# Shared homes for keys, values and folded sums, and 1280 instead of 768 columns of one output unit kept in SBUF

## Chip, cores and metric

One core of a Trainium2 chip. The metric is the device time of one launch in microseconds, the median of several runs. The core's engines are TensorE (PE, with its weight loads shown as PEld), VectorE (DVE), ScalarE (ACT), GpSimd (POOL) and SyncE (SP), and 16 DMA engines move data between HBM and SBUF. [...]

## What is computed

A layernormed input of 2048 rows goes through two branches, whose results are added to the input: a dense network with GELU, and an attention with a recurrent memory. The second is what this text is about: 64 segments of 32 rows, and eight memory rows that each segment takes from the output of the one before it.

```python
for s in range(n_seg):                       # 64, one after the other
    h = concatenate([mem, xs])               # 8 + 32 rows of 1024
    q, k, v = h @ Wq, h @ Wk, h @ Wv         # each 1024 x (32 heads x 128)
    p = softmax(mask(q @ k.T * scale))
    o = (p @ v) @ Wo                         # 4096 x 1024
    mem = o[:8]
    outs.append(o[8:])
return x + concatenate(outs) + dense(xn)
```

In bfloat16 the four weights hold 32 MB. They are read again in each segment, and not all of them fit in SBUF beside the rest.

## The kernel before

**Stages.** Until about 427 us the layernorm and the dense network run. They leave, for each segment, its turned rows and its residual in HBM. Then comes the recurrence, one segment after the other.

**Units.** The four weights are cut into 64 units of 128 x 2048 (512 KB): for each of K, Q and V eight slices of the model dimension in two halves u of 16 heads, and 16 units of Wo, two heads of the 32 each. `ORDER` is the order of use: K half 0, Q half 0, K half 1, Q half 1, V half 0, V half 1, output. 46 units stay in SBUF. 18 are marked S in `PLACED`. Two of these (`KEPT`) lie in four PSUM banks, from which VectorE copies them into a slot (L246). The other 16 are streamed from HBM in every segment by SP, through six slots: `unit_done` (L699) gives a slot back when the unit's matmuls are issued, and `start_stream` (L248) starts the next transfer into it. That transfer waits until TensorE has read the slot. One streamed output unit, `PART`, is partly resident: its first `PART_COLS` columns lie in `half_home`, only the rest is streamed (L257) into the right-hand part of the slot. `PART` is output unit 13 of 16.

**Left rows.** A segment's turned input has 32 columns: 24 of its rows (NX) and the eight memory rows. The last eight rows of each segment ("left" rows) are gathered over four segments (GRP) into a group of 32 and multiplied apart, each product in another segment of the group. With i4 = s mod 4: left K half 0 in i4 = 3 and half 1 in i4 = 0, left Q halves in 1 and 2, left V halves in 0 and 3, left outputs in 1. Where a pass has a left product, each unit is used twice, so its time doubles.

**A half pass** (`half_pass`, L757) goes through the eight units of a half. For each, `product` (L733) issues four matmuls of 128 x 512 with 32 columns of weights, in four column tiles of TensorE (L739). After a unit it may call functions that are listed for that step in `at`: so small work is put between the units by hand. The accumulators are three PSUM banks, `acc`; `mixed` is one more bank for scores, sums, masks and the memory.

**From pass to values.** A K or Q half is copied out of PSUM by ScalarE (`rows_out`, L790) and turned by VectorE (L804, L1007). `scores(u)` (L840) multiplies keys by queries into `mixed` (L848 for the segment, L854 for the left rows), takes Exp on ScalarE into `pr_all` (L860) and masks on VectorE (L867). `sums(u)` (L870) sums over the keys with small matmuls (L875, L881), takes Ln and two Exp on ScalarE (L886, L889) and multiplies on VectorE into `pd_main` (L896) and `pd_left` (L900). A V half is copied out of PSUM by ScalarE (`values_out`, L794). `values(u, rs)` (L907) multiplies it by `pd` (L915, L921) and copies the result out, r = 0 on ScalarE and r = 1 on VectorE (L929), into `outs[u]`. Output units 0 to 7 read the outputs of u = 0, units 8 to 15 those of u = 1 (`o_product`, L944, matmuls L962). In segments without left outputs, units 0 to 8 sum up in column-tile pairs, which `fold` (L971) adds between units 8 and 9 into `folded`. At the end `o_sb` is made (L1081 or L1084), `put_mem` (L284) writes the memory rows into the next segment's input, and the residual is added (L1104).

**Homes.** `d_oL` and `b_oL` (1024 columns each) are the outputs of u = 0 and u = 1: 64 columns for each of 16 heads, of which 32 are for left rows and the rest for the segment's. While they are not yet outputs, parts of them serve as `nat_home` (columns 32 to 63 of each head in `d_oL`: keys of half 1, and `o_sb`) and `q_home` (columns 24 to 63 in `b_oL`: queries). One more tile of 512 columns, tag "a", holds in turn the keys of half 0, the values of half 0, the values of half 1, and the folded sums. `hr_home` holds the turned rows and the residual of a segment.

**Order around the change.** In a segment: K0, Q0, K1, then the Q1 pass with scores(0) after its step 0 and sums(0) after step 6; V0, whose copy follows at once; the V1 pass with scores(1) after step 0, values(0) after step 1 and sums(1) after step 4 (in i4 = 3, where the pass is double: values(0) in two parts after 1 and 3); the output units with values(1) after unit 5 (in two parts after 4 and 6 where V1 has left products).

Of the kernel before, what the change touches and what calls it, by code (L numbers as in the profile page):

```python
# [57 lines left out]
PART_COLS = 768  # L58
# [31 lines left out]
def kernel(  # L90
# [49 lines left out]
    half_home = nc.alloc_sbuf_tensor_at("half_home", [P, DM], BF16, offset=SCRATCH)  # L140
    hr_home = nc.alloc_sbuf_tensor_at("hr_home", [P, 512], BF16, offset=SCRATCH + 2048)
    pd_main = nc.alloc_sbuf_tensor_at("pd_main", [P, 320], BF16, offset=SCRATCH + 3072)

    part_home, pr_all, res_home = half_home[:, 0:PART_COLS], half_home[:, PART_COLS:DM], hr_home[:, 256:512]
# [5 lines left out]
    pd_left = consts.tile([P, 128], BF16, name="pd_left")  # L150
# [66 lines left out]
    def fetch(t, unit):  # L217
        w, i, u = unit
        if unit == PART:
            h = 4 * i + 2 * u  # L220
            nc.sync.dma_start(out=t[:, 0:DM - PART_COLS], in_=Wo_v[:, h, PART_COLS:])
            nc.sync.dma_start(out=t[:, DM - PART_COLS:], in_=Wo_v[:, h + 1, :])
# [57 lines left out]
    b_oL = sp.tile([P, 1024], BF16, name="b_oL")  # L280
    outs = [t.rearrange("p (h t) -> p h t", h=16) for t in (d_oL, b_oL)]
    nat_home, q_home = outs[0][:, :, 32:64], outs[1][:, :, 24:64]
# [19 lines left out]
    with tc.tile_pool(name="ma", bufs=2) as ma, tc.tile_pool(name="mps", bufs=6, space=PSUM) as mps:  # L302
# [95 lines left out]
        def keep_xT(tg, xnT):  # L398
            xl = [sp.tile([P, 2, KT, GRP, NL], BF16, name="xl", tag=("a", "kL0")[k]) for k in range(2)]
# [28 lines left out]
        def turn_R(ttg, eng, small=None):  # L428
# [3 lines left out]
            for i in range(4):  # L432
# [8 lines left out]
                if with_left(seg):  # L441
                    m0 = main_row(slot)
# [4 lines left out]
                if seg < 2:  # L447
                    rows_at.append(NL * (slot ^ 2))
                elif seg >= NSEG - 2:
                    rows_at.append(main_row(1) + SEG + NL * slot)  # L450
# [64 lines left out]
        for tg in range(4):  # L515
            last = tg == 3
            if last:
# [4 lines left out]
                nc.sync.dma_start(out=half_home[:, :], in_=Wo_v[:, h, :])  # L522
# [122 lines left out]
    with tc.tile_pool(name="late", bufs=1) as late, \  # L645
# [69 lines left out]
        for s in range(NSEG):  # L715
# [14 lines left out]
            m0 = main_row(slot)  # L730
# [75 lines left out]
            def turn_k(ps, u):  # L806
                st["kT", u] = sp.tile([P, 16, 32], BF16, name="kT", tag="a")[:, :, :]
                turn(ps, st["kT", u], nc.scalar.copy)
# [31 lines left out]
            def scores(u, meanwhile=None):  # L840
# [4 lines left out]
                for c in range(4):  # L845
# [6 lines left out]
                    for j in range(4):  # L852
# [5 lines left out]
                        )  # L858
                pr = pr_all[:, 0:224]
# [10 lines left out]
            def sums(u):  # L870
# [17 lines left out]
                for b in (1, 0):  # L888
# [5 lines left out]
                pdB = pd_left.rearrange("p (c b a q) -> p c b a q", c=4, b=2, q=NL)  # L894
# [5 lines left out]
                nc.vector.tensor_tensor(  # L900
                    out=pdB.rearrange("p c b a q -> p b c a q"),
                    in0=prB.rearrange("p c (a q) -> p c a q", q=NL)[:, None, :, :, :].to_broadcast([P, 2, 4, 2, NL]),
# [106 lines left out]
            if not first:  # L1009
                at[6] = [lambda: sums(0)]  # L1010
# [164 lines left out]
```

## Time and profile before

| what | value |
|---|---|
| median of 3 runs | 1844.56 us (1840.67 to 1846.51) |
| the profiled execution | 1839.26 us, its span 1837.5 us |
| TensorE clock granted, mean | 0.996 |
| PE busy | 1717.9 us, 93% |
| PEld / DVE / ACT / POOL busy | 49% / 52% / 36% / 15% |
| until the recurrence, 0 to 427 us | DMA share 0.50, 157 GB/s |
| recurrence, 427 to 1837.5 us | DMA share 1.00, 387 GB/s |
| DMA queue of SP | 588.05 MB of 612.94 MB |

The share of a busy engine is an average. For the recurrence it has to be read from its own stretch, by segment or by group of four segments, since the four segments of a group do different amounts of left work. Matmuls overlap in the records. A DMA share over 1 means that packets overlap a little at their ends. In a list of waits a row gives engine, line and tile, what it waited for, the sum in us, how often, and the longest.

### The profile page before, as it was taken

The page shows a single profiled execution, that of the slowest core. Times are in us where ns is not written, and L with a number is a line of the kernel's source. Part 1 is how long each engine was busy: PE and PEld are TensorE (multiplying, and loading weights), DVE is VectorE, ACT ScalarE, POOL GpSimd, SP SyncE. Part 2 cuts the span into 40 slices and gives each one's busy share as a digit, 9 for nine tenths or more (in the row PEclk, how much of TensorE's full clock was granted, in tenths as well). Part 3 has the DMA queues.
Part 4 walks back from the last instruction along what each step waited for, and adds up shares of the span by engine and source line. Part 5 has one row for each costly group of instructions (what it writes and reads, how often), then busy time and mean ns, then how long its engine had stood idle before and what let it go on. Part 6 is the DMA issues. An engine that isn't in the chain of part 4 may idle for free.

```text
span 1837.5 us, 69927 instructions
## 1 busy us (share of the span) xinstructions
PE 1717.9 (93%) x30556; PEld 893.2 (49%) x30576; DVE 955.3 (52%) x2330; ACT 663.8 (36%) x1429; POOL 284.4 (15%) x559
## 2 busy tenths in 40 slices
PE   8999999998999999999999999999999999999997
PEld 4444444444454445454545545454545454545444
DVE  7657483805454545555454555455545454545543
ACT  6334251602333333333333333333333333333333
POOL 0000001501342111111111111112111111111111
PEclk9999999999999999999999999999999999999999
DMA  9931212769999999999999999999999999999998
GB/s 286 313 98 46 55 44 57 260 209 371 397 404 389 391 384 389 381 394 388 373 397 386 400 385 394 374 390 401 389 384 390 383 398 391 397 376 384 389 393 313
DMA packets 229278, 612.94 MB, mean 334 GB/s; under 512 B 46795, under 2 KB 76027, under 8 KB 228972
## 3 DMA queue, kind: packets, MB, share of 16 engines
q1 hardware_dynamic: 207252, 588.05, 84.3%
q0 software_dynamic: 17408, 17.69, 3.0%
q8 instruction: 239, 3.92, 0.8%
q10 hardware_dynamic: 4312, 2.73, 0.5%
q14 instruction: 67, 0.55, 0.1%
HBM read 594.40 MB, written 29.23 MB: 339 GB/s over the span
## 4 chain that ended last, share of the span: by engine, by line
PE 32%; DMA 18%; DVE 4%; ACT 2%; issue 1%; POOL 0%; DVEq 0%; ACTq 0%; SPq 0%
PE acc L739 22%; DMA u<-Wc_K 10%; PE acc L962 6%; DMA outL_d<-half_home 3%; DMA u<-Wc_O 3%; ACT mixed L889 1%; DVE b_oL L804 1%; PE acc L915 1%; DMA hr_home<-hr_d 1%; DVE pd_main L896 1%; PE mixed L848 1%; DMA u<-Wc_V 1%; ACT mixed L886 1%; DMA u<-Wc_Q 0%; PE mixed L854 0%
## 5 line engine op out<-in xcount | busy, mean ns | idle before, releaser
L739 PE MATMUL acc<-u,hr_home 128*32 128x512 bf16 x11520 | 770.8, 380 | 34.0 <-DMA u<-Wc_K 18.2
L739 PEld LDWEIGHTS <-hr_home 128*32 128x32 bf16 x12288 | 342.1, 96 | 317.3 <-issue 57.3
L739 PE MATMUL acc<-u,hrL 128*32 128x512 bf16 x2880 | 248.8, 379 | 3.0 <-DVE folded L978 3.0
L468 PE MATMUL ps<-u 128*128 128x512 bf16 (+1 forms) x920 | 195.7, 375 | 2.0 <-ACT u L388 2.0
L246 DVE TENSOR_SCALAR u<-kept 128x512 uint32<-128x512 uint32 x254 | 163.5, 685 | 35.4 <-PE acc L962 12.3
L962 PE MATMUL acc<-u,d_oL 128*32 128x512 bf16 (+1 forms) x1792 | 153.3, 381 | 11.7 <-DMA u<-Wc_O 9.4
L790 ACT CAST kT<-acc 128x512 bf16<-128x512 f32 x64 | 37.4, 585 | 307.6 <-PE acc L739 307.5
L589 PE MATMUL ps<-u 128*128 128x512 bf16 x657 | 146.2, 379 | 0.8
L962 PEld LDWEIGHTS <-b_oL 128*32 128x32 bf16 (+1 forms) x3381 | 108.4, 98 | 74.5 <-issue 35.9
L896 DVE TENSOR_TENSOR pd_main<-half_home,mixed 128x320 bf16<-128x320 bf16 x128 | 62.4, 487 | 153.2 <-ACT mixed L889 153.2
L468 PEld LDWEIGHTS <-u 128*128 128x128 bf16 x920 | 90.5, 99 | 105.5 <-issue 2.4
L1137 POOL DMA_DIRECT2D out_dram<-hr_home x188 | 96.3, 512 | 294.1 <-DVE hr_home L1104 280.5
L962 PE MATMUL acc<-u,b_oL 128*32 128x256 bf16 (+2 forms) x2062 | 117.1, 289 | 20.2 <-DMA u<-Wc_O 19.5
L804 DVE STREAM_TRANSPOSE b_oL<-b_oL 128x512 bf16<-128x512 bf16 x128 | 90.6, 708 | 64.8 <-ACT b_oL L790 64.8
L268 POOL DMA_DIRECT2D hr_home<-hr_d x58 | 32.8, 565 | 581.3 <-PE acc L739 576.1
L962 PEld LDWEIGHTS <-d_oL 128*32 128x32 bf16 (+1 forms) x2048 | 70.3, 99 | 84.7 <-issue 28.0
L739 PEld LDWEIGHTS <-hrL 128*32 128x32 bf16 x3072 | 82.9, 96 | 51.2 <-issue 7.7
L790 ACT CAST b_oL<-acc 128x512 bf16<-128x512 f32 x128 | 75.1, 587 | 86.1 <-PE acc L739 86.1
L589 PEld LDWEIGHTS <-u 128*128 128x128 bf16 x672 | 65.3, 98 | 77.3 <-DVE g_u L550 0.4
L889 ACT ACTIVATE mixed<-mixed,small_consts 128x160 f32<-128x160 f32 x256 | 94.2, 368 | 8.4
L542 ACT ACTIVATE g_xb<-ps,b1col 128x512 bf16<-128x512 f32 x112 | 76.8, 686 | 55.5 <-PE ps L468 54.7
L794 ACT CAST v<-acc 128x512 bf16<-128x512 f32 x128 | 75.1, 587 | 48.9 <-PE acc L739 48.6
(129 smaller groups left out, 2011.6 us busy)
## 6 DMA issues: line engine op xcount, KB each, us to landing
u<-Wc_K SPq DMA_DIRECT2D x320, 512.0 KB
u<-Wc_V SPq DMA_DIRECT2D x256, 512.0 KB
u<-Wc_O SPq DMA_DIRECT2D x256, 512.0 KB
u<-Wc_Q SPq DMA_DIRECT2D x128, 512.0 KB
u<-Wc_O SPq DMA_DIRECT2D x64, 320.0 KB
u<-in_B_w_dram SPq DMA_DIRECT2D x28, 512.0 KB
hr_home<-hr_d POOLq DMA_DIRECT2D x58, 128.0 KB, 5.5
u<-in_A_Wq_dram SPq DMA_DIRECT2D x14, 512.0 KB
```

The costliest lines, as they stand in the source:

```text
L246: nc.vector.tensor_single_scalar(out=out, in_=in_, scalar=0, op=ALU.bitwise_or)
L468: nc.tensor.matmul(ps[:, SEG * s0:SEG * s1].rearrange("p (s t) -> p s t", t=SEG), lhsT=w1_sb[fb // 2][:, kt, (fb % 2) * P:(fb % 2 + 1) * P ...
L542: nc.scalar.activation(out=xb[:, :], in_=ps[:, :], func=ACT.Identity, bias=b1col[:, fb:fb + 1], scale=1.0)
L589: nc.tensor.matmul(ps[:, :], lhsT=gts[fc // 4][:, fc % 4, t * P:(t + 1) * P], rhs=w2_sb[fc // 2][:, fc % 2, cs], start=(fc == 0), stop=(fc ...
L739: nc.tensor.matmul(o, lhsT=lhs[:, i, :], rhs=m, start=(i == seq[0]), stop=(i == seq[-1]), tile_position=(0, 32 * j),)
L790: cp(out=out, in_=ps.rearrange("p (h e) -> p h e", e=32))
L794: cp(out=t[:, :], in_=ps[:, :])
L804: nc.vector.transpose(out=home, in_=home)
L889: nc.scalar.activation(out=mixed[:, 160 * b:160 * b + 160], in_=mixed[:, 0:160], func=ACT.Exp, scale=-1.0, bias=off[:, b:b + 1],)
L896: nc.vector.tensor_tensor(out=pdA.rearrange("p c b q -> p b c q"), in0=prA[:, None, :, :].to_broadcast([P, 2, 4, 40]), in1=dd, op=ALU.mult,)
L962: nc.tensor.matmul(acc[r0:r0 + rows, c:c + wide], lhsT=lhs[:, 4 * (i % 4) + 2 * u + k, :], rhs=cols, start=start, stop=stop, tile_position ...
L1137: nc.gpsimd.dma_start(out=out_flat[rows, 256 * j:256 * j + 256], in_=res[32 * j:32 * j + NX, :])
```

## The change

It moves the homes and some steps, and lets more columns of `PART` stay.

- `PART_COLS` is 1280 instead of 768. `half_home` has 1536 columns (1280 for the unit, 256 for `pr_all`); `hr_home` moves to another pool. The streamed rest of `PART` is 768 columns.
- The tag "a" is gone. Keys of half 0 and the folded sums go to `nat_home`. `b_oL` is replaced by `q_all` (640 columns) and `left_outs` (512, left outputs of u = 1). Values of both halves, the segment's outputs of u = 1 (`outM`) and `o_sb` share columns 0 to 511 of `q_all` with the queries, one after the other; in i4 = 3 the values of half 1 lie in `kL[1]`.
- `pd_left` is gone: for u = 1 it is in columns 512 to 639 of `q_all`, for u = 0 in a part of `left_outs`, written by two products instead of one.
- scores(0) is issued after the last unit of K1 instead of after step 0 of Q1; its Exp and masks, now `exps`, come before K1's copy. sums(0) comes after step 4 instead of 6, but for i4 = 2.
- V0's copy is issued after the matmuls of scores(1) and before its Exp (`attend`). values(0) comes after step 4, sums(1) after step 6; in i4 = 3 values(0) after 3 and 5, sums(1) after 5, values(1) after units 5 and 7.
- For u = 1 the copy out of `values` has two parts, left rows and segment rows. In segments with left outputs the later eight output units use 32 columns of weights from each of two tiles instead of 64 from one.

```diff
-PART_COLS = 768
+PART_COLS = 1280
...
-    half_home = nc.alloc_sbuf_tensor_at("half_home", [P, DM], BF16, offset=SCRATCH)
-    hr_home = nc.alloc_sbuf_tensor_at("hr_home", [P, 512], BF16, offset=SCRATCH + 2048)
+    half_home = nc.alloc_sbuf_tensor_at("half_home", [P, PART_COLS + 256], BF16, offset=SCRATCH)
...
-            nc.sync.dma_start(out=t[:, 0:DM - PART_COLS], in_=Wo_v[:, h, PART_COLS:])
-            nc.sync.dma_start(out=t[:, DM - PART_COLS:], in_=Wo_v[:, h + 1, :])
+            nc.sync.dma_start(out=t, in_=Wo_v[:, h + 1, PART_COLS - DM:])
...
-    b_oL = sp.tile([P, 1024], BF16, name="b_oL")
-    outs = [t.rearrange("p (h t) -> p h t", h=16) for t in (d_oL, b_oL)]
-    nat_home, q_home = outs[0][:, :, 32:64], outs[1][:, :, 24:64]
+    left_outs = sp.tile([P, 512], BF16, name="left_outs")
+    q_all = sp.tile([P, 640], BF16, name="q_all")
+    outs0, outL = d_oL.rearrange("p (h t) -> p h t", h=16), left_outs.rearrange("p (h t) -> p h t", h=16)
+    v_home = q_all[:, 0:512]
+    outM = v_home.rearrange("p (h t) -> p h t", h=16)
+    nat_home, q_home = outs0[:, :, 32:64], q_all.rearrange("p (h t) -> p h t", h=16)
...
             def turn_k(ps, u):
-                st["kT", u] = sp.tile([P, 16, 32], BF16, name="kT", tag="a")[:, :, :]
-                turn(ps, st["kT", u], nc.scalar.copy)
+                st["kT", u] = nat_home
+                turn(ps, nat_home, nc.scalar.copy)
...
+                if u:
+                    pdB = q_all[:, 512:640].rearrange("p (c b a q) -> p c b a q", c=4, b=2, q=NL)
+                else:
+                    pdB = outL[:, :, 24:32].rearrange("p (c b a) q -> p c b a q", c=4, b=2)
...
-                    out = outs[u][:, 8 * r:8 * r + 8, NL * slot:NL * slot + 40]
-                    cp(out=out.rearrange("p (b c) q -> p c b q", b=2), in_=oV[r])
+                    h = slice(8 * r, 8 * r + 8)
+                    if u == 0 and m0 == NL * slot + NL:
+                        parts = [(outs0[:, h, NL * slot:NL * slot + 40], 0, 40)]
+                    else:
+                        parts = [
+                            ((outL if u else outs0)[:, h, NL * slot:NL * slot + NL], 0, NL),
+                            (outM[:, h, :] if u else outs0[:, h, m0:m0 + SEG], NL, 40),
+                        ]
+                    for out, q0, q1 in parts:
+                        cp(out=out.rearrange("p (b c) q -> p c b q", b=2), in_=oV[r][:, :, :, q0:q1])
...
                     if left_o:
-                        tiles = [(64 * r, 64, (2 * r, 2 * r + 1)) for r in range(2)]
+                        lhs = [(0, 32, outL[:, h, :]), (32, 32, main)] if i >= 4 else [(0, 64, outs0[:, h, :])]
+                        tiles = [(64 * r + r0, w, (2 * r, 2 * r + 1), lhsT) for r0, w, lhsT in lhs for r in range(2)]
...
-                t = sp.tile([P, 256], F32, name="folded", tag="a")
+                t = nat_home.bitcast(F32)
...
-            psK1, psK1L = half_pass("K", 1, left_k[1], {})
+            psK1, psK1L = half_pass("K", 1, left_k[1], {7: [lambda: scores(0)]})
+            exps(0, None if first else lambda: q_left(1))
             st["kT", 1] = nat_home
             rows_out(psK1, nat_home, nc.scalar.copy)
             at = {
-                0: [lambda: scores(0, None if first else lambda: q_left(1)), lambda: nc.vector.transpose(out=nat_home, in_=nat_home)],
+                0: [lambda: nc.vector.transpose(out=nat_home, in_=nat_home)],
             }
             if not first:
-                at[6] = [lambda: sums(0)]
+                at[6 if i4 == 2 else 4] = [lambda: sums(0)]
...
-            st["V", 0] = values_out(psV, sp.tile([P, 512], BF16, name="v", tag="a"), nc.scalar.copy)
...
-            at = {0: [lambda: scores(1)], 4: [lambda: sums(1)]}
+
+            def attend():
+
+                scores(1)
+                st["V", 0] = values_out(psV, v_home, nc.scalar.copy)
+                exps(1)
+
+            at = {0: [attend]}
             if left_v[1]:
-                at.update({1: [lambda: values(0, (0,))], 3: [lambda: values(0, (1,))]})
+                at.update({3: [lambda: values(0, (0,))], 5: [lambda: values(0, (1,)), lambda: sums(1)]})
             else:
-                at[1] = [lambda: values(0, (0, 1))]
+                at.update({4: [lambda: values(0, (0, 1))], 6: [lambda: sums(1)]})
...
-            st["V", 1] = values_out(psV1, sp.tile([P, 512], BF16, name="v", tag="a"), nc.scalar.copy)
+            apart = left_v[1] and not first
+            v1 = kL[1].rearrange("p h t -> p (h t)") if apart else v_home
+            st["V", 1] = values_out(psV1, v1, nc.scalar.copy)
...
-                o_sb = nat_home
+                o_sb = outM
```

## The prediction

> **What bounds the kernel now.** I read the slices first, then the busy row of a long stretch of the recurrence, then who waits for whom, then the timeline of one segment.
>
> ```profile
> PE   8999999998999999999999999999999999999997
> ...
> PEclk9999999999999999999999999999999999999999
> DMA  9931212769999999999999999999999999999998
> ```
>
> From about slice 10 on the 64 segments run, with TensorE and the 16 DMA engines both at nine tenths. The first 427 us are layernorm and the dense network, which the change hardly enters. To part the two, the row for 506 to 1735 us (56 segments, 14 groups of four):
>
> ```profile
> core 0: us, PE busy (x) PEld busy (x) DVE busy (x) ACT busy (x) POOL busy (x), PEclk, DMA share, GB/s
> ...
> 506.20:1735.00 1228.80, 1141.80 (x25054) 613.65 (x25046) 626.40 (x1512) 439.65 (x1023) 206.96 (x395) 1.00 1.01 389
> ```
>
> A group takes 1228.8/14 = 87.8 us. TensorE is busy for 81.6 of it and idle for 6.2. The DMA share is 1.01; cut into slices of 1 us, the packet records give 1.027 on three slices of four, so 1.027 is "full" and the engines miss only 1.6 us a group. DMA work alone is 86.2 us a group. What TensorE waits for (600 to 1800 us):
>
> ```profile
> PE acc L962 <- DMA u<-Wc_O: 24.8, 51, 1.3
> PE acc L739 <- DMA u<-Wc_K: 17.1, 30, 1.9
> PE mixed L848 <- DVE b_oL L804: 10.1, 37, 0.4
> ```
>
> The first two are 41.9 us in 1200, or 3.1 us a group. So TensorE with its own waits needs 87.8 - 3.1 = 84.7 us a group, DMA 86.2, and the group takes 87.8: **the weight stream binds, with TensorE 1.5 us a group behind it.** By segment (i4 = s mod 4): nearly all DMA waits come late in i4 = 0 (its last products and the next segment's first keys) and late in i4 = 2; i4 = 1 and 3, which do more left products, have next to none.
>
> Here the Trainium skill (Perfetto Trace Analysis, Identifying the Most-Contended Engine) speaks for a choice: matmul busy time is no measure of headroom, because matmuls are pipelined. By the busy row (93%) TensorE would be the bound and the removed bytes worth nothing; by the rule that row proves nothing, and the PEld row (50%) leaves room. By the row the sum below would be +14 us (the new TensorE waits alone), by the rule -11. The DMA share and the waits side with the rule.
>
> **Removed bytes.**
>
> ```profile
> u<-Wc_O SPq DMA_DIRECT2D x64, 320.0 KB
> ```
>
> This transfer becomes 192 KB, the other 15 per segment (512 KB) stay. Its 128 packets shrink from 2560 to 1536 bytes. The trace's packet records give 105 ns (mean) for the first size and 65 ns for the second (it occurs in the load phase). Eight packets per engine: 8 x 40 = 0.32 us a segment, x64 = **20.6 us**, or 1.3 us a group; 128 KB at 389 GB/s would be 0.34. Once, in segment 0, 128 KB more are loaded (+0.3 us); in the load phase 128 KB less are copied, beside TensorE work.
>
> **Moved keys.** scores(0) now stands one unit (four matmuls, 0.217 us) earlier. It had 0.32 to 0.76 us between the end of the query transpose and its start, needs 0.05: free. Exp now precedes the copy of K1; that copy feeds only scores(1), some 4 us later. In i4 = 2 Exp waits for a left-output DMA as before, and K1's copy and the transpose wait behind it; the next taker of that PSUM bank is V0, a double pass (3.5 us) later: free. sums(0) is two units earlier in i4 = 0, 1, 3, so net one unit nearer to scores(0): 1.32 us instead of 1.54, with the mask ready 1.20 us after scores(0) starts (1.33 in i4 = 3): at most 0.06 us of wait, in i4 = 3. The gain: Ln, two Exp and then Q1's copy on ScalarE run earlier, and scores(1), which waits for that query transpose (the L804 row above), gets it some 0.23 us sooner in i4 = 1. In i4 = 0 and 3 a left-key copy (0.59) stands before Ln, and the split `pd` product costs VectorE two of about 0.18 (96- and 64-element L867: 198 and 180 ns) instead of one of 0.28, so nothing is gained: +0.1 in i4 = 3. Folded sums in `nat_home` and outputs in `v_home` keep engine and size: nothing.
>
> **Values, where waits are added.** ScalarE in V1/O of an i4 = 0 segment:
>
> ```profile
> 1058.20 0.29 ACT L886 ACTIVATE mixed<-mixed 128x160 f32<-128x160 f32 x1 [0.51 <-PE mixed L881]
> 1058.52 0.77 ACT L889 ACTIVATE mixed<-mixed,small_consts 128x160 f32<-128x160 f32 x2
> 1059.21 0.59 ACT L794 CAST v<-acc 128x512 bf16<-128x512 f32 x1
> 1060.46 0.42 ACT L929 CAST b_oL<-acc 128x320 bf16<-128x320 f32 x1 [0.66 <-PE acc L921]
> ```
>
> and TensorE at the same place:
>
> ```profile
> 1057.82 0.24 PE L875 MATMUL mixed<-half_home,small_consts 128*32 128x160 bf16 x4
> ...
> 1059.97 0.21 PE L915 MATMUL acc<-pd_main,v 64*128 64x80 bf16 x2
> ...
> 1061.03 0.62 PE L962 MATMUL acc<-W_O,b_oL 128*32 128x512 bf16 x12
> ```
>
> V0's copy must now wait until scores(1) has read the queries, and it stands ahead of Exp on ScalarE. Exp(1), its masks and sums(1) queue behind it: Exp moves by about 0.55 us. sums(1) stands two units later (0.43) and had 0.33 to 0.5 us of slack, so it just fits; values(0), at step 4, meets the copy within 0.05 us. Then the chain: sums(1) at 1057.82 to values(1) at 1059.97 is 2.15 us, set by ScalarE (Ln, two Exp, V1's copy, ending at 1059.80). Before, nine units and the sums (2.05 us) lay beside it; now seven (1.62). **TensorE waits 0.43 us more** in i4 = 0. In i4 = 2 as much, where DMA waits of about 0.7 us already lie in that stretch. In i4 = 1 the doubled output units cover it; in i4 = 3 the distance is kept. In i4 = 1 the later read of `pr_all` also holds the left residual's load on the POOL queue (L1072) back by 0.43 us; it lands 5.0 us after its issue and is used 6.1 us or more after: covered, and what is queued behind it on POOL (output stores) feeds nothing in the segment.
>
> Last, values(1)'s copy becomes two, 64 and 256 elements, left part first, and output unit 8 waits for the second. A 256-element copy is 368 ns (L975), a 512-element one 587: 0.86 ns an element over 148 ns, so 64 make 203 ns. The sum is 571 against 425: +0.15 us without overlap. The Trainium skill (ScalarE: Activation LUTs, What ACT_TABLE_LOAD costs) has 186 ns + 0.833 ns an element, with back-to-back ones overlapping by 93 ns: 239 + 399 - 93 = 545 against 453, +0.09. The Exp rows show 30 ns between neighbours, not an overlap; I take +0.15, in i4 = 0, and 0.1 in i4 = 2. The other two have slack for it.
>
> Left outputs: in 17 segments the eight later output units issue eight matmuls with 32 columns instead of four with 64, in four column tiles instead of two. A key unit with four such tiles runs at 0.217 us, a 64-wide pair of k at 0.22: zero; from -0.1 to +0.3 us per such segment, as no trace row shows that order.
>
> **Sum per group:** TensorE +0.43 + 0.15 + 0.43 + 0.1 - 0.23 + 0.1 - 0.1 (values(0) no longer tight) = +0.9; DMA -1.3. TensorE 84.7 becomes 85.6, DMA 86.2 becomes 84.9. Most of the +0.9 falls where DMA waits follow, and shortens those. Two nearly equal paths through six buffers overlap less well than a plain maximum says: before the group stood 1.6 above the higher, I take 1.5 again, 87.1. Gain 0.7 x 16 = **11 us**: 1839.3 becomes 1828 in a profiled run. The median of the runs shown is 5 us above that execution, so 1844.6 - 11 = **1833 us**. What a measurement can tell from no change is 0.3%, 5.5 us.
>
> **Rivals.**
> - Bytes at full value: all new waits fall into DMA waits. 1844.6 - 20.6 = 1824. For it: 3.1 us a group of such waits against 0.9. Against: i4 = 1 and 3 have none to give.
> - Even: TensorE becomes the bound from its +0.9, and the group stays at 87.5 to 88: 1839 to 1848. For it: the margin of 1.5 us. Against: DMA waits still 1.5 after my sum.
> - Slower: V0's copy cannot hide. If the copy (0.59 us, behind scores(1), ahead of Exp) comes out as a TensorE wait at sums(1) or values in all four segments, the TensorE path is 85.6 + 4 x 0.59 = 88.0, above the old group even with no DMA waits; with 0.7 us of them left it is 88.7, +0.9 a group: 1859. It decides from 0.55 us a segment on. Against: my 0.2 us of slack before sums(1), small as it is.
>
> **Numbers.** Forecast (-6 to -17) 0.42; full value 0.18; even 0.17; slower 0.23. So faster 0.60, same 0.17, slower 0.23. The range goes from 1820 to 1856; the forecast's own is 1827 to 1839.
>
> **To look for after.** The smaller transfer 64 times; DMA waits of TensorE falling from 3.1 to about 1.5 us a group; values(1) some 0.5 us later than its turn in i4 = 0; scores(1)'s wait for the queries smaller; DMA share still about 1. I am wrong if sums(1) or values(0) show TensorE waits of several tenths in every segment, or if the DMA share falls below 0.98.

## The result and the profile after

The changed kernel takes **1845.8 us** (median of 22 runs, 1840.6 to 1866.7), the kernel before, run beside it, 1843.5 (22 runs, 1837.8 to 1853.4). The ratio is 1.0016 with a 95% interval of 0.9997 to 1.0035: no change that can be told. I had forecast 1833. The profiled execution after took 1846.56 us, its span 1844.8, at a granted clock of 0.994 (0.996 before). It is 7 us above the profiled execution before, where the medians are 2 us apart; of the small differences between these two profiles below, some may be of the execution and not of the kernel.

The slices, and the row of the transfer that was to shrink, on the page of the kernel after:

```profile
PE   8999999999898899999999999999899998989997
...
DMA  9931212769999999999999999999999999999997
...
u<-Wc_O SPq DMA_DIRECT2D x64, 192.0 KB
```

The bytes are gone: the transfer has 192 KB instead of 320, and the SP queue moves 579.67 MB instead of 588.05. The DMA row still stands at nine tenths or more throughout, while the PE row now has eights in it. The row for the same long stretch of the recurrence (columns as in the row of the prediction):

```profile
506.00:1735.00 1229.00, 1135.47 (x25404) 609.63 (x25400) 637.82 (x1619) 431.25 (x1072) 207.36 (x395) 1.00 1.00 381
```

The DMA share is 1.00, where it was 1.01, at 381 GB/s instead of 389. TensorE is busy 1135.5 us instead of 1141.8. So in the same time the stream moves fewer bytes, and its engines look as full as before. Who waits for whom, 600 to 1800 us:

```profile
PE acc L991 <- DMA u<-Wc_O: 23.7, 51, 1.6
PE acc L991 <- DVE q_all L956: 15.6, 14, 1.2
PE acc L744 <- DMA u<-Wc_K: 9.8, 24, 1.3
PE mixed L859 <- issue: 5.5, 6, 2.4
...
PE mixed L853 <- DVE q_all L809: 3.3, 12, 0.3
```

L991 is the output product (L962 before), L744 the product of the passes (L739), L956 the copy out of `values` (L929), L853 the scores (L848). The two rows of waits for weights fell from 41.9 to 33.5 us. The wait of scores for the turned queries fell from 10.1 to 3.3. But the second row is new: 14 waits of 1.1 us, one in each segment with i4 = 3, for VectorE's copy of values(1).

By segment, from one `put_mem` to the next, means of 14 groups:

```
i4               0      1      2      3     group
before       20.74  23.89  21.01  22.08     87.72 us
after        21.26  23.40  20.63  22.68     87.97 us
```

i4 = 1 and 2 gained 0.87 us together, i4 = 3 and the following i4 = 0 lost 1.12. Ahead of these groups two segments lost 4.3 us once (21.5 and 23.0 became 23.9 and 24.9); one wait of 3.1 us for VectorE's copies at L245 stands there, where the longest was 1.2 before.

### The profile page after: what moved, and what is told of

Its sections match the earlier page's. It is cut to its first block, busy times and chain, and to the rows that moved or that the text cites. A ratio compares the mean times of both kernels' runs of the same rounds, so it can differ in the third digit from the quotient of the medians.

```text
span 1844.8 us, 71272 instructions
## 1 busy us (share of the span) xinstructions
PE 1716.7 (93%) x31117; PEld 889.9 (48%) x31137; DVE 971.4 (53%) x2459; ACT 657.3 (36%) x1494; POOL 284.6 (15%) x559
## 3 DMA queue, kind: packets, MB, share of 16 engines
q1 hardware_dynamic: 207252, 579.67, 83.3%
## 4 chain that ended last, share of the span: by engine, by line
PE 66%; DMA 26%; DVE 3%; ACT 2%; issue 2%; POOL 0%; DVEq 0%; ACTq 0%; SPq 0%; POOLq 0%
PE acc L744 29%; DMA u<-Wc_K 12%; PE ps L473 10%; PE acc L991 10%; PE ps L594 8%; DMA u<-Wc_V 5%; DMA u<-Wc_O 5%; DMA outL_d<-half_home 2%; DMA u<-Wc_Q 2%; PE ps L627 2%; PE acc L934 2%; ACT mixed L897 1%; PE mixed L853 1%; DVE q_all L809 1%; PE pT L627 1%
## 5 line engine op out<-in xcount | busy, mean ns | idle before, releaser
L744 PE MATMUL acc<-u,hr_home 128*32 128x512 bf16 x11520 | 775.2, 381 | 27.4 <-DMA u<-Wc_K 10.9
L744 PEld LDWEIGHTS <-hr_home 128*32 128x32 bf16 x12288 | 341.5, 96 | 317.9 <-issue 61.3
L744 PE MATMUL acc<-u,hrL 128*32 128x512 bf16 x2880 | 249.2, 380 | 2.7 <-issue 2.4
L245 DVE TENSOR_SCALAR u<-kept 128x512 uint32<-128x512 uint32 x254 | 163.6, 686 | 50.3 <-PE acc L991 29.9
L795 ACT CAST d_oL<-acc 128x512 bf16<-128x512 f32 x128 | 74.6, 583 | 297.5 <-PE acc L744 297.5
L991 PE MATMUL acc<-u,d_oL 128*32 128x512 bf16 (+1 forms) x1792 | 153.7, 382 | 17.3 <-DMA u<-Wc_O 13.5
L991 PEld LDWEIGHTS <-q_all 128*32 128x32 bf16 x3381 | 101.1, 97 | 54.7 <-issue 23.1
L991 PE MATMUL acc<-u,q_all 128*32 128x256 bf16 (+1 forms) x1951 | 111.6, 292 | 16.0 <-DMA u<-Wc_O 15.8
L809 DVE STREAM_TRANSPOSE q_all<-q_all 128x512 bf16<-128x512 bf16 x128 | 90.6, 708 | 64.8 <-ACT q_all L795 64.8
L991 PEld LDWEIGHTS <-d_oL 128*32 128x32 bf16 (+1 forms) x2048 | 70.3, 99 | 89.0 <-issue 43.1
L799 ACT CAST q_all<-acc 128x512 bf16<-128x512 f32 x113 | 66.3, 587 | 127.9 <-PE mixed L859 124.8
L744 PEld LDWEIGHTS <-hrL 128*32 128x32 bf16 x3072 | 83.7, 96 | 49.4 <-issue 5.5
L795 ACT CAST q_all<-acc 128x512 bf16<-128x512 f32 x128 | 75.2, 587 | 87.0 <-PE acc L744 87.0
```

The costliest lines, as they stand in the source:

```text
L245: nc.vector.tensor_single_scalar(out=out, in_=in_, scalar=0, op=ALU.bitwise_or)
L744: nc.tensor.matmul(o, lhsT=lhs[:, i, :], rhs=m, start=(i == seq[0]), stop=(i == seq[-1]), tile_position=(0, 32 * j),)
L795: cp(out=out, in_=ps.rearrange("p (h e) -> p h e", e=32))
L799: cp(out=t[:, :], in_=ps[:, :])
L809: nc.vector.transpose(out=home, in_=home)
L991: nc.tensor.matmul(acc[r0:r0 + rows, c:c + wide], lhsT=lhsT, skip_group_check=True, rhs=cols, start=start, stop=stop, tile_position=(0, r0),)
```

## Where the new wait comes from

VectorE in a segment with i4 = 3, first in the kernel before, then in the kernel after (start us, duration us, engine, line, operation):

```profile
1040.04 0.49 DVE L929 CAST b_oL<-acc 128x320 bf16<-128x320 f32 x1 [1.74 <-PE acc L921]
1040.77 1.29 DVE L246 TENSOR_SCALAR u<-kept 128x512 uint32<-128x512 uint32 x2 [0.23 <-DMA u<-Wc_O]
1041.97 0.84 DVE L978 TENSOR_TENSOR folded<-acc,folded 64x256 f32<-64x256 f32 x2
```

```profile
1045.01 1.29 DVE L245 TENSOR_SCALAR u<-kept 128x512 uint32<-128x512 uint32 x2 [1.55 <-PE acc L991]
1046.21 0.21 DVE L956 CAST left_outs<-acc 128x64 bf16<-128x64 f32 x1
1046.35 0.41 DVE L956 CAST q_all<-acc 128x256 bf16<-128x256 f32 x1
1046.68 0.84 DVE L1012 TENSOR_TENSOR d_oL<-acc,d_oL 64x256 f32<-64x256 f32 x2
```

and TensorE in the kernel after:

```profile
1045.31 0.40 PE L991 MATMUL acc<-W_O,q_all 128*32 128x512 bf16 x4
1046.82 0.40 PE L991 MATMUL acc<-W_O,q_all 128*32 128x256 bf16 x8 [1.11 <-DVE q_all L956]
```

`unit_done` of output unit 7 gives a slot back, and the unit that falls into that slot is a `KEPT` one, so VectorE copies it out of PSUM: 1.29 us (L246, now L245). Before, the second part of values(1) came after unit 6, and its copy stood ahead of these two. The change moves it to unit 7, behind `unit_done`, and so behind 1.29 us of copying: VectorE takes its work in the order in which it is issued, and the copy starts at 1046.21, as the second of these two ends (1046.30). At unit 9 `new_acc` takes the next of three PSUM banks in turn, which is the bank that values(1) has just filled; the fold stands in between, and TensorE waits for the copy.

## The experiments

Each ran beside the kernel before, on the same chip; ratios are to it. The kernels from e5 on, but for e11, leave a part of the weights out and read another part twice in its place, so they compute only a part of the result; they are there for their times.

**1. The late step by itself, and with the bytes (e1 to e4).** e1 is the kernel after with the steps of `values(1)` put back; e2 is the kernel before with the late step alone; e3 is the kernel after with 768 columns; e4 has both edits of e1 and e3.

```diff
 # e1, e4: kernel after, i4 = 3
-                at = {5: [lambda: values(1, (0,))], 7: [lambda: values(1, (1,))], 9: [lambda: left_values(1, psV1L)]}
+                at = {4: [lambda: values(1, (0,))], 6: [lambda: values(1, (1,))], 9: [lambda: left_values(1, psV1L)]}
 # e2: kernel before
-                at = {4: [lambda: values(1, (0,))], 6: [lambda: values(1, (1,))]}
+                at = {4: [lambda: values(1, (0,))], 6 if first else 7: [lambda: values(1, (1,))]}
 # e3, e4: kernel after
-PART_COLS = 1280
+PART_COLS = 768
 ...
```

> The changed kernel with one thing put back: in i4 = 3 the two parts of values(1) come after output units 4 and 6, as before, instead of 5 and 7. Theory A (VectorE's copy of the second part stands behind two stash copies of 0.69 us each that unit 7 starts, and output unit 9 waits for that copy's PSUM bank, 1.1 us in each i4 = 3 segment): that TensorE wait goes, and the time falls by 8 to 17 us against the changed kernel, to about 1829 to 1837, 0.992 to 0.997 of the kernel before. Theory B (what eats the saved bytes are the waits at values(1) and output unit 8 in i4 = 0 and 2, where TensorE now binds): within 4 us of the changed kernel. Theory C (fewer streamed bytes are worth nothing whatever the waits are): also at the time of the kernel before, ratio 1.00.

> The kernel before with only this moved: in i4 = 3 the second part of values(1) comes after output unit 7 instead of 6. Theory A: TensorE waits about 1.1 us on VectorE in each i4 = 3 segment (15 of them), and the time grows by 8 to 17 us, ratio 1.004 to 1.009. Theory B: no change, ratio 1.00, as the weight stream covers a wait of TensorE.

> The changed kernel with 768 resident columns as before, so with the homes and steps of the change alone and 320 KB in the partly streamed transfer. If the bytes are worth their full price, it is 20 us slower than the changed kernel, ratio to before about 1.012. Theory A: 8 to 20 us slower than the changed kernel, ratio 1.006 to 1.013. Theory C: the same as the changed kernel, ratio about 1.001.

> 768 resident columns, and in i4 = 3 the two parts of values(1) after output units 4 and 6: the change without its saved bytes and without the late step. Theory A: near the kernel before, ratio 0.998 to 1.005 (the small waits of i4 = 0 and 2 against the earlier queries of i4 = 1), and e1 is 8 to 20 us faster than this. Theory B: as slow as the changed kernel with 768 columns, since the waits at values(1) in i4 = 0 and 2 are still there. Theory C: the same as e1.

Measured, ratio with its interval:

```
                     768 columns                        1280 columns
late step      e3 1.0050 [1.0032, 1.0067]        after 1.0016 [0.9997, 1.0035]
early step     e4 1.0010 [0.9994, 1.0027]        e1    1.0007 [0.9987, 1.0027]
e2 (before + late step)  1.0033 [1.0017, 1.0050]
```

The late step does what the timeline says. In e1, without it, TensorE's wait for this copy is gone. In e2 the same row appears in the kernel before, between the same neighbours:

```profile
PE acc L962 <- DMA u<-Wc_O: 21.7, 50, 1.3
PE acc L962 <- DVE b_oL L929: 15.7, 14, 1.1
PE acc L739 <- DMA u<-Wc_K: 14.5, 31, 1.3
```

It is 15.7 us of waits, but costs 6 us (e2) or 7 us (e3 against e4). The rows for weights are 5.7 us smaller than in the kernel before, so a part of the wait stands where a wait for weights stood; the profiled execution of e2, 1840.8 us, was the shortest of its 15, so the rest cannot be read from it. The other half surprised me: the 128 KB are worth about 6 us where the late step is (e3 to the kernel after), and nothing where it isn't (e4 to e1). At 1280 columns the late step costs only some 2 us, where I had expected e1 to gain 8 to 17: even without the late step the change is at 1.0007. So the late step does not explain the forecast that was missed; the bytes do. The difference of these differences is about as large as the intervals allow, so I take from it no more than this: the bytes do not bring 11 us in any pair. And e4 at 1.001 is the price of all other moved steps together: some 2 us, give or take 3.

**2. The bytes by themselves (e5, e6, e8, e10).** All start from the kernel before. e5 shortens the transfer of `PART` to 192 KB (`copies[unit][:, 512:]`) and reads 512 resident columns twice, e6 cuts a quarter of one streamed V unit, e8 a quarter of all four, e10 drops one V transfer whole.

```diff
 # e6, e8: in start_stream; product reads the second quarter twice
-            nc.sync.dma_start(out=t[:, :], in_=copies[unit])
+            c = 512 if cut(unit) else 0
+            nc.sync.dma_start(out=t[:, c:], in_=copies[unit][:, c:])
 ...
 # e10: in start_stream; the product reads a resident unit
+        while n >= STREAMED and streams[n] == ("V", 6, 1):
+            stream_tiles[n], slot_of[n] = res_tiles[RESIDENT[0]], None
+            ...
+            n = starts.popleft()
 ...
```

> The kernel before, with only the streamed bytes of the change: the partly streamed transfer has 192 KB instead of 320 KB in each segment; its product reads 512 resident columns twice in place of the 512 that are not loaded, so that part of the result is left wrong. Theory P (full price of bytes on a saturated stream): 20 us faster, ratio 0.989. Theory D (this transfer runs while TensorE is in the V1 and output units; in i4 = 1 and 3 the six slots are then full and the DMA engines pause anyway, so the saving is lost in a longer pause, and only in i4 = 0 and 2 can it reach a TensorE wait): 0 to 8 us faster, ratio 0.996 to 1.000, with more DMA pauses in i4 = 1 and 3. Theory S (the turnover of slots, not bytes, sets the pace): no change, ratio 1.000, for this and for the next two kernels.

> The kernel before, with the same 128 KB a segment taken from another transfer: the last streamed V unit loads 1536 of its 2048 columns, and its product reads one column block twice. Theory P: 20 us faster as well. Theory D: this transfer comes ahead of the output units at which TensorE waits in i4 = 0 and 2, so it is worth more than the same bytes in the partly streamed unit: 8 to 16 us faster, ratio 0.991 to 0.996. Theory S: no change.

> The kernel before, with 512 of 2048 columns left out of all four streamed V units (512 KB a segment; their products read a column block twice). Full price would be 4 x 20 = 82 us, but TensorE's own path (84.7 of 87.8 us a group) allows about 50. Theory P: 45 to 50 us faster, ratio 0.973 to 0.976. Theory D: 20 to 40 us faster, ratio 0.978 to 0.99. Theory S: no change.

> The kernel before without one streamed V transfer after segment 0 (its product reads a resident unit): 512 KB less a segment, the same as with a quarter of four transfers left out, which gave 10 us, but also one slot use less of 18. Theory S: clearly more than those 10 us, 15 to 30 us faster, ratio 0.984 to 0.992. If bytes alone count: 10 us, ratio 0.9945.

```
                                  us       ratio
e5   -128 KB, PART             1844.4   1.0019 [1.0000, 1.0038]
e6   -128 KB, one V            1840.3   0.9994 [0.9977, 1.0012]
e8   -512 KB, in four V        1833.6   0.9952 [0.9934, 0.9971]
e10  -512 KB, one V transfer   1823.2   0.9896 [0.9858, 0.9934]
```

So the edit that I had priced at 20.6 us of DMA time, made alone, gains nothing (e5 is 0 to 7 us slower), and not because of what this change moves. Nor is it the place of these bytes alone: e6 takes as many elsewhere, and lies between 4 us faster and 2 slower. 512 KB cut in quarters give 9 us of 82; the same 512 KB as one whole transfer, which also takes one of 18 uses of a slot away, give 19.

**3. What TensorE needs without the stream (e7).** The kernel before, with the seven streamed K and Q units read from a resident one after segment 0:

```diff
+        while n >= STREAMED and streams[n] in copies and streams[n][0] in "KQ":
+            stream_tiles[n], slot_of[n] = res_tiles[RESIDENT[0]], None
 ...
```

> The kernel before without the seven streamed K and Q transfers after segment 0: their products read one resident unit instead, all other work stays. 44% of the streamed bytes go, so what is left is the path of TensorE with its own waits. By the sum of the prediction (84.7 us of 87.8 a group) the time falls by about 50 us, ratio 0.973. If TensorE binds already and its DMA waits only stand in for other waits (theory T), less than 15 us, ratio above 0.992.

1757.7 us, 0.955 [0.9524, 0.9576]. The row of e7 for 506 to 1700 us:

```profile
506.00:1700.00 1194.00, 1148.30 (x25862) 612.95 (x25862) 633.88 (x1560) 452.24 (x1055) 207.65 (x396) 1.00 0.69 235
```

The DMA share is 0.69, and a group takes 82.5 us. So TensorE's own path is at most 82.5 us, not the 84.7 that I had. Its busy time fell too, from 81.6 to 79.4 us a group for the same 1789 matmuls, of which those with 512 columns last 380 ns on average in both. So some 2 us of "busy" in the kernel before were time between matmuls, in pieces that no row shows. What held them up is not shown.

**4. Slots instead of bytes (e9, e12 to e16).** e16 is the kernel before with five stream slots, e9 and e13 with seven. The seventh takes the place of one resident output unit.

```diff
 # e13; e9 leaves LATER at 3; e16 has 5 slots and LATER = 2
-LATER = 3
+LATER = 4
-STREAM_BUFS = 6
+STREAM_BUFS = 7
-    RING = ["xn0", "xn1", "w1_0", "w1_1", "xn2", "xn3"]
+    RING = ["xn0", "xn1", "w1_0", "w1_1", "w1_2", "xn2", "xn3"]
 ...
+        res_tiles[LATE[0]] = res_tiles[RESIDENT[0]]
 ...
```

> The kernel before with seven slots for streamed units instead of six. The room comes from one late output unit, which is not kept and reads another resident unit in its place (that part of the result is left wrong); bytes and number of transfers stay. Theory S (neither the engines' bytes nor TensorE binds alone; the hand-over through six slots does, and part of the DMA engines' busy time is waiting inside packets): 15 to 40 us faster, ratio 0.978 to 0.992, with fewer packets over 300 ns. Theory P (a saturated stream): a further slot adds no bandwidth, less than 6 us, ratio above 0.997.

> Seven slots as in the run before it, and 192 KB instead of 320 KB in the partly streamed transfer (its product reads 512 resident columns twice). Theory S: with the hand-over relaxed the stream is nearer to its real limit, so the 128 KB are worth more than with six slots, 5 to 15 us against the run with seven slots alone. If bytes are worth nothing here either (within 4 us), what is saved is lost in the packets' waiting whatever the slots are.

e9 was 1.0062 [1.0038, 1.0085], e12 (e9 with the bytes of e5) 1.0079 [1.0044, 1.0113], so slower, where I had expected e9 15 to 40 us faster. I had overlooked VectorE once more. With seven slots and `LATER` = 3 the copies out of PSUM fall before the last addition of the segment, and in e9 the first matmul of `put_mem` stands for it:

```profile
PE mixed L291 <- DVE d_oL L1085: 42.4, 38, 1.4
PE acc L963 <- DMA u<-Wc_O: 13.7, 31, 1.2
```

Of waits for weights 1.1 us a group are left of 3.1, but the wait above stands in their place, so e9 tells nothing for or against the slots. The next three set `LATER` to one more, and e16 to one less.

> The kernel before with seven stream slots instead of six and LATER = 4 instead of 3; the seventh slot takes the place of one resident output unit, whose product reads another resident unit's weights. Every transfer starts as many slots ahead as there are slots, and the two stash copies keep the place in VectorE's order that they had with six slots, which e9 did not. Slots theory (the hand-over through six slots sets the pace, both engines having about 5 us of slack in a group of four segments): VectorE's wait before the memory rows is gone again, the waits of TensorE for DMA stay as low as in e9 (about 1.1 us a group), and the time falls 15 to 35 us, to 1808-1828. Full-stream theory (the transfers' bytes bind and slots only shift the wait): within 5 us of before.

> e13 with 128 KB less in each transfer of the partly resident output unit, as e5 has it. If with seven slots the stream's bytes bind, it gains up to 20 us on e13. If TensorE's own order binds by then, within 3 us of e13. Slots theory expects the second.

> e13 with a quarter less in each of the four value transfers (512 KB a segment, as e8). With six slots this gave 9 us of a full price of 82. Slots theory: with a seventh slot TensorE alone binds, at no less than the 82.5 us a group of e7; together with e13's gain the time is 1775-1815. Full-stream theory: about e8's 1834.

> The kernel before with five stream slots instead of six and LATER = 2, nothing else. Slots theory: the reach ahead falls by a sixth and the waits of TensorE for DMA grow; 25 to 80 us slower. Full-stream theory: the stream is at work all the time with five slots too, and the time is within 10 us of before.

```
                                                                a group: length   waits of TensorE for
                              us       ratio                             weights  VectorE  "issue"
e16  5 slots              1894.3   1.0259 [1.0220, 1.0299]      90.83      4.13     4.66     0.42
before, 6 slots           1842.8                                87.72      3.07     1.56     1.17
e13  7 slots              1832.1   0.9950 [0.9928, 0.9971]      87.40      0.50     2.27     3.17
e14  7, -128 KB           1835.4   0.9950 [0.9924, 0.9975]      87.29      0.51     2.32     3.17
e15  7, -512 KB in four   1822.2   0.9884 [0.9851, 0.9917]      86.27      0.22     2.72     2.06
e5   6, -128 KB           1844.4   1.0019 [1.0000, 1.0038]      87.97      2.40     2.28     1.43
e10  6, 1 transfer less   1823.2   0.9896 [0.9858, 0.9934]      86.70      0.94     1.77     2.16
e7   6, 7 transfers less  1757.7   0.9550 [0.9524, 0.9576]      82.47      0.48     2.47     0.07
```

Lengths and waits (those over 0.15 us) are means over 14 groups of each kernel's one profiled execution. e5 shows where its saved bytes went: waits for weights fell by 0.67 us a group, and 0.72 of waits for VectorE and 0.26 of "issue" stand there instead.

One slot less costs about 50 us with the same bytes, at a DMA share still 1.00 (377 GB/s). But e16 is no clean measure of slots: its group is 3.1 us longer, with 3.1 more of waits for VectorE, whose copies out of PSUM have moved once more, and only 1.1 more of waits for weights, against 0.75 less of "issue". e13 is cleaner, though its waits for VectorE grow by 0.7. Nearly all its waits for weights are gone, 2.6 us a group, yet the group is only 0.3 us shorter in its profile, and the time about 10 us, less than the 15 I had expected at the least. What took their place is seen in the waits of e13, 600 to 1740 us:

```profile
PE acc L740 <- issue: 15.8, 26, 1.1
PE acc L963 <- issue: 12.2, 18, 1.8
PE acc L963 <- DVE b_oL L930: 9.4, 14, 0.7
PE acc L740 <- DVE hr_home L295: 9.1, 16, 1.2
PE mixed L849 <- DVE b_oL L805: 9.0, 30, 0.4
PE mixed L849 <- issue: 6.9, 11, 1.2
PE acc L963 <- DMA u<-Wc_O: 3.5, 10, 0.6
```

"issue" means that the profile shows nothing TensorE waited for. The packet records show something. The page lists a queue named "instruction" (q8), and its packets of 16 KB take about 1.0 us each. In the kernel before it has 239, and TensorE has 61,132 matmuls and weight loads, 256 to a packet, so I take the queue for TensorE's. I took every "issue" wait of TensorE over 0.25 us in 506 to 1735 us and looked how long before its end the last of these packets had landed. In the kernel before these are 29 waits (16 us), and all 29 end 1.20 to 1.70 us after such a landing. In e13 they are 64 (42 us), all between 1.20 and 1.62 us. A random moment would lie in so narrow a span about one time in twelve. In e7 there is one such wait, in e16 there are ten. So what these waits follow is the arrival of instructions.

With five, six and seven slots they are 0.42, 1.17 and 3.17 us a group, which looks like an effect of the slots. It need not be: e10 has six slots and 512 KB less to stream in each segment, and 2.16 us of them, its largest row of waits (600 to 1750 us):

```profile
PE acc L746 <- issue: 15.0, 19, 1.4
PE mixed L855 <- DVE b_oL L811: 9.0, 31, 0.4
PE acc L746 <- DMA u<-Wc_K: 8.3, 15, 1.2
```

What e10 and e13 share is that TensorE waits less for weights. In e5, e10, e13, e14, e16 and the kernel before the waits for weights and for instructions together are 3.1 to 4.6 us a group; in e15 they are 2.3, and only in e7, with seven of 16 transfers gone, are both nearly away. So instructions may come late in all of these, and show where no wait for weights covers it; that is a reading, and no run tests it. Whether the instruction packets queue behind the weights isn't shown: the records hold no time of request, and the packets themselves take 1.0 us in e7 too. The Trainium skill (Runtime: NRT & Kernel Launch, Instruction fetch mechanics) has instructions fetched in blocks of 16 KB and calls the cost of crossing from one block to the next "mostly hidden"; the block size agrees, but here up to 3.2 us of an 87 us group are not hidden.

e14 prices this change's 128 KB at nothing with seven slots, too. e15 is about 10 us faster than e13, as e8 is 9 faster than before, and lies above the 1775 to 1815 that I gave it. So half of the theory that the slots set the pace falls: with a slot more TensorE hardly waits for weights, but other waits stand in for these, and the bytes have the same small price with six slots and with seven.

**5. One repair on top (e11).** e1 with sums(1) after step 5 instead of 6, against the wait in the i4 = 0 segments.

> The changed kernel with values(1) of i4 = 3 back at units 4 and 6, and sums(1) after step 5 instead of 6 of the V1 pass in the other segments. It shortens TensorE's wait at values(1) by 0.2 us in i4 = 0 and 2. If such a wait costs the 0.4 us per us that the late step cost: 2 to 4 us faster than the first alone, ratio to before 0.998 to 1.000. If it is covered: no change against it.

1844.5 us, 0.9996 [0.9973, 1.0019]: nothing. No kernel that computes the whole result came out faster than the one before.

## Why full DMA engines were not the bound

I read a share of 1.01 as a stream with nothing to spare. The packet records of the SP queue, 506 to 1735 us, say otherwise. The 4096-byte packets (GB/s and share of e8 and e7 up to 1700 us, where their last segments end earlier):

```
                    GB/s  share   median    mean     99%
before               389   1.01   159 ns   167.0     420 ns
e1                   382   1.00   159      168.5     441
e8                   367   0.98   159      173.2     579
e7                   235   0.69   159      188.7     701
```

GB/s and share are those of all queues. With fewer bytes the median packet stays at 159 ns, but more packets take far longer. In e5 the packets of `PART` use 17 us less of the stretch (47 to 30, summed over the 16 engines and divided by 16), and the 4096-byte packets 2 to 10 us more in the kernels with those bytes gone (1122.6 becomes 1124.3 in the kernel after, 1128.8 in e1, 1132.2 in e5). The share therefore holds more than a packet's 159 ns, and what it holds more grows when bytes go: it stays near 1 while GB/s falls. The Trainium skill (Perfetto Trace Analysis, Identifying the Most-Contended Engine) says to look at HBM utilization rather than at the occupancy of DMA engines. Here the two parted: GB/s followed the bytes, 389 to 381, and the share did not. But GB/s would have warned no better beforehand, with 389 on average and 398 in the median microsecond of the kernel before. What the slow packets wait for, no run here shows.

The queue that starts the transfers shows how the two paths hang together. In the kernel before, 600 to 1800 us, SP waits for TensorE to have read a slot (waits for L739, L962 and the small matmuls together: 701 us, 811 times, for some 875 transfers):

```profile
SPq L259 <- PE acc L739: 417.0, 506, 2.1
SPq L259 <- PE acc L962: 139.0, 179, 3.2
```

So nearly every transfer starts when TensorE lets it, and TensorE waits 83 times for a transfer. My sum compared the two as if each ran alone.

## The prediction, step by step

- **"In i4 = 3 the distance is kept"** is the step that failed on the loss side. I counted TensorE's distance from sums(1) to values(1) and did not follow values(1)'s copy into VectorE's queue, past which the move to unit 7 carries it. I put this term at nothing; it is 15.6 us of waits, and 6 to 7 us of time at 768 columns (e2, e3 against e4), some 2 at 1280 (e1). It explains the smaller part of the miss.
- **"1.027 is 'full' and the engines miss only 1.6 us a group"** is the step that failed on the gain side, and it decides: without the late step the change still gains nothing (e1, 1.0007). With it falls "TensorE 84.7, DMA 86.2". I took the DMA engines' busy time as the length of their work, took 1.3 us a group from it, let TensorE's 85.6 become the longer path, and came to 0.7 us a group, 11 us. The runs have no gain that can be told for these bytes by themselves (e5 1.0019, e6 0.9994, e14 equal to e13; some 6 us beside the late step, e3 to the kernel after), a busy share that stays when bytes go, and a path of TensorE of at most 82.5 us (e7). The reading itself was generous: the share lies between 1.02 and 1.035 on 64% of the slices of 1 us, not on three of four. What I have in its place is argued and not shown: two paths that wait for each other through six slots, the VectorE copies and the instructions make 87.7, so that 1.3 us less on one of them moves the waits and not the end.
- **"By the row +14, by the rule -11"**: neither came, it is +2. The busy row was no bound, as the rule has it: in e7 the group is 5.2 us shorter with all of TensorE's work in it. But room on TensorE did not make the bytes worth their price.
- **Removed bytes, 0.32 us a segment:** the size of the step was right as DMA work: the packets of `PART` fell from 105 to 66 ns.
- **Scores(0) for nothing, sums(0) earlier:** right. Scores(0) keeps at least 0.12 to 0.56 us after the query transpose, by segment, and never waits for it; the wait of scores(1) for queries went in i4 = 1 (5.2 us became none in the list, so up to 0.37 a segment where I had 0.23), and in i4 = 3 too (2.4 us), where I had expected no gain.
- **Values(1) waits 0.43 us more in i4 = 0:** right in kind, too large. TensorE's work between sums(1) and values(1) is 1.62 us, the chain takes at least 2.04. That leaves 0.42, where 0.10 stood before, so 0.32 more; in six of the 14 segments late weights or instructions cover a part of it or all. The list has 1.7 us for it, in seven of 14. In i4 = 2 other waits cover it, as I had it.
- **The copy in two parts, +0.15:** too large. ScalarE's parts lie over each other by 0.10 us, and the pair ends 0.06 later than the one copy did (0.69 against 0.63 us from the start of the last matmul). I had added the durations, and had missed that the list I showed has such an overlap: the Exp pair ends at 1059.29, V1's copy starts at 1059.21.
- **The sum, +0.9 us a group on TensorE:** e4 has all of these without late step or bytes and costs 2 us, give or take 3, where 0.9 in each of 16 groups would be 14 if TensorE bound. So most of it lay beside other waits.
- **Rivals.** The time fell into the even case, 1839 to 1848, but by luck and not by its reason: e5 has none of those waits on TensorE and is at 1.0019 all the same. The slower case needed 0.55 us a segment from V0's copy; Exp(1) moved by 0.43 us (0.55 forecast), and sums(1) mostly fitted with 0.33 us or more to spare.
- I wrote that a DMA share under 0.98 would show me wrong. It stayed at 1.00, and I was wrong all the same: the sign was badly chosen.

ScalarE after, in an i4 = 0 segment, with Exp(1) close behind V0's copy and the overlapping parts at the end:

```profile
1062.31 0.58 ACT L799 CAST q_all<-acc 128x512 bf16<-128x512 f32 x1 [3.58 <-PE mixed L859]
1062.79 0.36 ACT L868 ACTIVATE half_home<-mixed 128x224 bf16<-128x224 f32 x1
...
1066.51 0.21 ACT L956 CAST left_outs<-acc 128x64 bf16<-128x64 f32 x1 [0.66 <-PE acc L940]
1066.62 0.38 ACT L956 CAST q_all<-acc 128x256 bf16<-128x256 f32 x1
```

and TensorE there, values(1) after its wait, and a wait for weights behind it:

```profile
1065.91 0.21 PE L934 MATMUL acc<-pd_main,q_all 64*128 64x80 bf16 x2 [0.25 <-DVE pd_main L907]
...
1068.77 0.40 PE L991 MATMUL acc<-u,q_all 128*32 128x256 bf16 x8 [1.10 <-DMA u<-Wc_O]
```

**What stays open:** how much of 87.7 us is due to each of the couplings, what the slow packets wait for, and why the late step costs less at 1280 columns than at 768.

## To carry to other kernels

A step that is moved is moved in the queue of every engine that it feeds: list what `unit_done` or its like puts on that queue between the old place and the new, and ask which buffer the copy holds back. A busy share near one, of matmuls or of DMA engines, need not be a bound (93% and 1.01 here); take a part of that work away in an experiment before pricing it, above all where two paths hand over to each other through a few buffers. When one wait is removed, add up all kinds of idle time again: another supplier may be late next, the instructions among them.

## What was not expected of the hardware

- DMA busy time is not fixed by the bytes: seven of 16 transfers less made the mean 4096-byte packet slower, 188.7 instead of 167.0 ns, at an unchanged median of 159.
- TensorE stood up to 3.2 us a group in waits that go with the arrival of its instructions (e13), 2.2 with one transfer of 16 less (e10), 0.07 with seven less (e7); each such wait over 0.25 us in these and the kernel before ends 1.2 to 1.7 us after a 16 KB instruction packet has landed.
- TensorE's busy time shrank by 2 us a group without one matmul less (e7).
